# Two blocks of the w3 fold transposed by TensorE instead of VectorE

## The chip, the cores and the metric

The kernel runs on one core of a Trainium2 chip. The metric is the device time of one execution in microseconds (us); a lower one is better. Five engines run side by side, each through its own queue in program order: TensorE (PE in the views; PEld is its weight load), VectorE (DVE), ScalarE (ACT), GpSimd (POOL) and SyncE (SP, which here issues loads). "SPq" is SP's queue of DMA issues.

## The reference

Three layers follow each other: a kernelised attention over 8 heads, then a gated layer with four weight matrices, then a dense mixture of four experts. The change lies in the second.

```python
def _moe_ref(x, w1, w2, w3, w_out):
    a = x @ w1
    b = x @ w2
    h = a * b @ w3
    return (h @ w_out).astype(np.float32)
```

The sizes are x 1152x512, w1 and w2 512x1024, w3 1024x1024, w_out 1024x512. The weights arrive as float64.

## The kernel before

Since nothing stands between w3 and w_out, the kernel multiplies these two weights first ("the fold"): w3 @ w_out is 1024x512, half as wide as w3. It does this while the attention is still running, about 60 to 133 us into the span, in pieces that stand between the attention's own steps. The table `BESIDE` says which pieces go with which step; the framework's scheduler then sets the order of each engine's queue.

Every product here is done with numbers split in two float32r parts (HI and LO): three matmuls in place of one. `split` makes the parts: ScalarE copies the source to HI, VectorE subtracts HI from the source to get LO.

The fold needs w3 with its columns on the partitions, so w3 must be transposed. It has 8 row groups `m` of 128 rows, each cut in two halves `hf` of 512 columns: sixteen blocks, numbered u = 2m + hf. I call them u0 to u15. A block goes through these steps (line numbers of before):

1. SP loads it as float64, 512 KB, in four pieces of 32 partitions (L91), into one of six buffers `hx`.
2. ScalarE (L119, "the Prelu") and VectorE (L120 a shift, L121 an or) make it float32 in `w3f`, a tile of the tag `f64f`, which has two buffers.
3. VectorE transposes 32x32 squares (L257, STREAM_TRANSPOSE) from `w3f` to `w3t`. The four load pieces had put the rows where these squares give a whole transpose.
4. `split` makes `w3T` from `w3t`: ScalarE L83, VectorE L84. `w3T` has two buffers.
5. TensorE multiplies it with eight tiles of w_out: 12 matmuls of 128x512 a block (L274), 24 a fold of one `m`.

`fold(m)` sums in PSUM bank `po` for even m and `w` for odd m. The block ahead is prepared while the present one is multiplied. At the end of a fold `split` moves the bank's content into `w3o` (ScalarE L83, VectorE L84); only then may the bank be written again. During one fold the other fold's bank is the "spare bank".

Beside the fold run the attention steps of pairs 3 to 7: `features` (TensorE L394 into `ps_f`, VectorE L405 the maximum `mx`, ScalarE L407 eight exponentials `eq` or `ek`), transposes by TensorE (L134 into `ps_et` or `ps_x`), and the small products L360 and L565. After the fold come the gated products (L193, L224), which take what `load_w12` prepares, the expert input, and then the experts.

Of the kernel before, what the change touches and what calls it, by code (L numbers as in the profile page):

```python
# [10 lines left out]
F32R = mybir.dt.float32r  # L11
# [5 lines left out]
HI, LO = 0, 1  # L17
# [2 lines left out]
HALVES = 5  # L20
EARLY = 2
WARM = 6


PASSES = ((LO, HI), (HI, LO), (HI, HI))
# [21 lines left out]
def attention_moe_kernel(ctx: ExitStack, tc: tile.TileContext, q, k, v, omega, mw1, mw2, mw3, mwo, probs, ew1, ew2, out):  # L47
# [6 lines left out]
    P = 128  # L54
    SQ = 32
# [22 lines left out]
    def bank(tag):  # L78
        return ps_p.tile([P, 512], F32, tag=tag, name="ps_" + tag, bufs=BANKS[tag])

    def split(hi, lo, src, eng=None):

        high = nc.scalar.activation(out=hi, in_=src, func=ACTF.Copy)  # L83
        low = (eng or nc.vector).tensor_tensor(out=lo, in0=src, in1=hi.bitcast(F32), op=ALU.subtract)  # L84
        return high.ins, low.ins
# [8 lines left out]
    ahead, blocks = [], []  # L94

    def fetch(n):

        while len(ahead) < min(n, len(blocks)):
            r = hx_p.tile([P, 2, S], U32, tag="hx", name="f64").rearrange("p a s -> p (a s)")[:, :1024]
            ahead.append(load_f64(r.rearrange("p (c w) -> p c w", w=2), blocks[len(ahead)]))  # L100

    def next_block(name):

        n = next(turns)
        f = from_f64(ahead[n], name)
        fetch(n + 1 + HX_BUFS)
        return f
# [3 lines left out]
    def from_f64(r, name):  # L111


        low, high = r[:, :, 0], r[:, :, 1]
        f = cv.tile([P, 512], F32, tag="f64f", name=name, bufs=2)
        e = cv.tile([P, 512], U32, tag="f64e", name="f64e", bufs=2)
        fb = f.bitcast(U32)

        nc.scalar.activation(out=f, in_=high.bitcast(F32), func=ACTF.Prelu, scale=2.0**-112, alpha=2.0**32)  # L119
        nc.vector.tensor_scalar(out=e, in0=low, scalar1=29, scalar2=None, op0=ALU.logical_shift_right)  # L120
        nc.vector.scalar_tensor_tensor(out=fb, in0=fb, scalar=3, in1=e, op0=ALU.logical_shift_left, op1=ALU.bitwise_or)  # L121
        return f
# [10 lines left out]
    def transpose(out, in_, rows=slice(0, P)):  # L133
        return nc.tensor.transpose(out, in_, ident[rows, rows])  # L134
# [25 lines left out]
    cv = cctx.enter_context(tc.tile_pool(name="cv", bufs=2, side="right"))  # L160
# [80 lines left out]
    w3T = []  # L241
    for n in range(KF):
        hf, g = divmod(n, 4)
        blocks.append([mwo[hf * 512:(hf + 1) * 512].rearrange("(p g) d -> g p d", g=4)[g].unsqueeze(1)])
    for u in range(2 * KF):
        m, hf = divmod(u, KF // 4)
        rows = mw3[m * P:(m + 1) * P].rearrange("(j r) f -> r j f", r=SQ)
        blocks.append([rows[:, :, f:f + P] for f in range(hf * 512, hf * 512 + 512, P)])
    blocks += [[gated_columns(src, g)] for g in range(EARLY) for src in (mw1, mw2)]

    def fold_transposed(u):

        r = next_block("w3f")
        t = cv.tile([P, 512], U32, tag="f64e", name="w3t", bufs=2).bitcast(F32)
        nc.vector.transpose(t, r.rearrange("p (j c g) -> p j g c", j=4, g=4))  # L257
        t = t.rearrange("p (j g r) -> p g j r", j=4, g=4)
        wt = cv.tile([P, 2, 512], F32R, tag="w3T", name="w3T", bufs=2)
        hi, lo = (wt[:, x].rearrange("p (g j r) -> p g j r", j=4, g=4) for x in (HI, LO))  # L260
        split(hi, lo, t)
        w3T.append(wt)

    def fold(m):

        po = bank(("po", "w")[m % 2])
        n = 0
        for hf in range(KF // 4):
            u = m * (KF // 4) + hf
            while len(w3T) < min(u + 2, KF * (KF // 4)):  # L270
                fold_transposed(len(w3T))
            for g in range(4):
                for a, c in PASSES:
                    nc.tensor.matmul(  # L274
                        out=po, lhsT=w3T[u][:, a, g * P:(g + 1) * P], rhs=wo[hf * 4 + g][:, c],
                        start=(n == 0), stop=(n == 3 * KF - 1),
                    )
                    n += 1
        t = w3_p.tile([P, 2, 512], F32R, tag="w3o", name="w3o", bufs=KF)
        split(t[:, HI], t[:, LO], po)  # L280
        w3o.append(t)
# [57 lines left out]
    with ExitStack() as actx:  # L339
# [81 lines left out]
        ps = bank("po")  # L421
        for n in range(WARM):
            nc.tensor.matmul(out=ps, lhsT=zeros[:, :P], rhs=zeros, start=True, stop=True)
# [18 lines left out]
        for b in range(B):  # L442
            t = st.tile([P, H, D1], F32, name=f"vt{b}")
# [137 lines left out]
        def pair(n):  # L581
            return pairs[n] if 0 <= n < len(pairs) else None
# [34 lines left out]
        for n in range(len(pairs) + 1):  # L617
            u, u1, nx, nx2 = pair(n), pair(n - 1), pair(n + 1), pair(n + 2)
# [381 lines left out]
```

## Time and profile before

| | |
|---|---|
| median of 3 runs | 655.72 us (654.99 to 656.09) |
| the profiled execution | 656.22 us |
| its span, first to last instruction | 654.5 us |
| TensorE busy | 641.4 us, 98% of the span |
| VectorE busy | 460.8 us, 70% |
| ScalarE busy | 416.5 us, 64% |
| granted TensorE clock | 1.00 in all 40 slices |

The span is 1.7 us shorter than the execution's own time, which is what lies around it. The busy shares are means over stages with different limits. A TensorE that is busy is not at its peak, and its waits are few and short; so the stretches and the single waits have to be read.

### The profile page before, as it was taken

To read this page: it belongs to the slowest core of one execution; us is meant where nothing else is said; L and a number is where in the kernel's file an instruction comes from. 1 tells how busy PE (TensorE), PEld (TensorE's weight loads), DVE (VectorE), ACT (ScalarE), POOL (GpSimd) and SP (SyncE) were. 2 spreads that over 40 slices of the span, in tenths; PEclk is the share of its full clock that TensorE was granted. 3 is DMA by queue.
4 is the path that set the end of the run, shared out by engine and by line. 5 is a ranking of instruction groups with operands and counts; after the bars stand their busy time and mean duration, and the time that the engine had idled before them with its cause. 6 is when DMAs were issued, how large, how long until landed. Compare 5 with 4: busy or idle time off the path is not lost.

```text
span 654.5 us, 12627 instructions
## 1 busy us (share of the span) xinstructions
PE 641.4 (98%) x4971; PEld 609.8 (93%) x4971; DVE 460.8 (70%) x756; ACT 416.5 (64%) x892; POOL 122.6 (19%) x145
## 2 busy tenths in 40 slices
PE   8998999999999999999999999999999999999997
PEld 6787787789999999999999999999999999999997
DVE  3678987896623252657958968788598679687795
ACT  5899566664532242457868767778687677687750
POOL 2223000051310000000131330430422413314200
PEclk9999999999999999999999999999999999999999
DMA  9978662144200012002243672781783854836824
GB/s 258 326 192 229 167 166 70 34 129 146 81 0 1 1 66 65 1 2 65 64 138 106 106 134 69 151 153 19 146 146 46 150 111 83 140 86 96 165 63 146
DMA packets 58396, 70.61 MB, mean 108 GB/s; under 512 B 8864, under 2 KB 43680, under 8 KB 58336
## 3 DMA queue, kind: packets, MB, share of 16 engines
q1 hardware_dynamic: 44720, 48.79, 25.4%
q0 software_dynamic: 12640, 20.19, 20.4%
q8 instruction: 39, 0.64, 0.4%
q10 hardware_dynamic: 976, 0.82, 0.4%
q14 instruction: 21, 0.17, 0.1%
HBM read 47.24 MB, written 22.54 MB: 107 GB/s over the span
## 4 chain that ended last, share of the span: by engine, by line
PE 85%; ACT 5%; DVE 4%; DMA 3%; issue 2%; POOL 1%; SPq 0%; DVEq 0%; ACTq 0%; POOLq 0%
PE ps_f L823 7%; PE ps_f L908 6%; PE ps_et L823 3%; PE ps_po L823 3%; PE ps_w L823 3%; PE ps_x L823 3%; PE ps_kv L823 3%; PE ps_t L823 3%; PE ps_et L908 3%; PE ps_x L908 3%; PE ps_kv L908 3%; PE ps_w L908 3%; PE ps_t L908 3%; PE ps_po L908 3%; PE ps_f L224 3%
## 5 line engine op out<-in xcount | busy, mean ns | idle before, releaser
L857 POOL DMA_DIRECT2D out_dram<-o x98 | 82.1, 944 | 352.9 <-DVE o L883 170.1
L84 DVE TENSOR_TENSOR hs<-hd,hs 128x1024 fp32r<-128x1024 f32 x48 | 58.5, 1220 | 0.8 <-ACT hs L83 0.8
L83 ACT ACTIVATE hs<-hd 128x1024 fp32r<-128x1024 f32 x48 | 50.6, 1057 | 7.9 <-PE ps_et L908 2.5
L823 PE MATMUL ps_f<-x,w1e 128*128 128x288 f32 x288 | 46.9, 294 | 0.0
L807 ACT ACTIVATE hd<-hd 128x288 f32<-128x288 f32 x96 | 41.0, 437 | 7.9 <-DVE hd L805 7.3
L719 DVE TENSOR_TENSOR hd<-hd 128x512 f32<-128x512 f32 x64 | 44.0, 687 | 1.5 <-ACT hd L807 0.4
L719 DVE TENSOR_TENSOR raw<-raw 128x512 f32<-128x512 f32 x64 | 44.0, 687 | 0.6
L84 DVE TENSOR_TENSOR w2e<-raw,w2e 128x1024 fp32r<-128x1024 f32 x32 | 38.8, 1218 | 6.1 <-ACT w2e L83 6.0
L908 PE MATMUL ps_f<-w2e,hs 128*128 128x256 f32 x288 | 42.7, 282 | 0.0
L823 PEld LDWEIGHTS ps_f<-x,w1e 128*128 128x128 f32 x288 | 41.1, 188 | 0.2
L908 PEld LDWEIGHTS ps_f<-w2e,hs 128*128 128x128 f32 x288 | 38.2, 191 | 0.1
L83 ACT ACTIVATE w2e<-raw 128x1024 fp32r<-128x1024 f32 x32 | 32.9, 1056 | 6.1 <-DVE raw L719 3.7
L84 POOL TENSOR_TENSOR w<-w12f,w 128x512 fp32r<-128x512 f32 x16 | 22.2, 1396 | 67.9 <-ACT w L83 66.0
L84 DVE TENSOR_TENSOR w1e<-raw,w1e 128x1024 fp32r<-128x1024 f32 x24 | 29.3, 1222 | 4.4 <-ACT w1e L83 4.3
L83 ACT ACTIVATE hid<-a 128x192 fp32r<-128x192 f32 (+2 forms) x32 | 13.4, 441 | 27.0 <-DVE a L234 25.0
L83 ACT ACTIVATE w1e<-raw 128x1024 fp32r<-128x1024 f32 x24 | 25.4, 1060 | 4.6 <-DVE raw L719 2.9
L274 PE MATMUL ps_w<-wo,w3T 128*128 128x512 f32 x96 | 24.3, 400 | 2.3 <-DVE w3T L84 2.3
L376 DVE TENSOR_REDUCE mx<-ps_f 128x4 f32<-128x512 f32 x24 | 16.5, 689 | 13.7 <-PE ps_f L370 12.7
L274 PE MATMUL ps_po<-wo,w3T 128*128 128x512 f32 x96 | 24.0, 399 | 1.6 <-DVE w3T L84 1.6
L880 ACT ACTIVATE o<-ps_f,pr 128x256 f32<-128x256 f32 (+1 forms) x37 | 17.8, 482 | 9.9 <-PE ps_f L908 8.8
L823 PE MATMUL ps_et<-x,w1e 128*128 128x288 f32 x144 | 23.6, 295 | 0.0
L823 PE MATMUL ps_po<-x,w1e 128*128 128x288 f32 x144 | 23.6, 294 | 0.0
(307 smaller groups left out, 1709.7 us busy)
## 6 DMA issues: line engine op xcount, KB each, us to landing
raw<-in_moe_w_dram SPq DMA_DIRECT2D x32, 512.0 KB, 5.5
out_dram<-o POOLq DMA_DIRECT2D x56, 256.0 KB, 4.8
f<-in_moe_w_dram SPq DMA_DIRECT2D x64, 128.0 KB, 3.5
f<-in_moe_w_dram SPq DMA_DIRECT2D x16, 512.0 KB, 4.1
out_dram<-o POOLq DMA_DIRECT2D x42, 128.0 KB, 4.6
f<-in_moe_w_out_dram SPq DMA_DIRECT2D x8, 512.0 KB, 7.6
vr<-in_v_dram SPq DMA_DIRECT2D x8, 256.0 KB, 5.3
o<-out_dram SPq DMA_DIRECT2D x8, 256.0 KB, 5.3
```

What stands on the lines that cost most here:

```text
L83: high = nc.scalar.activation(out=hi, in_=src, func=ACTF.Copy)
L84: low = (eng or nc.vector).tensor_tensor(out=lo, in0=src, in1=hi.bitcast(F32), op=ALU.subtract)
L224: nc.tensor.matmul(out=ps[:, :third], lhsT=w12[w, g][:, x, kk], rhs=xb[kk][:, y, cols[c]], start=(kk == 0 and n == 0), stop=(kk == KD - 1 ...
L274: nc.tensor.matmul(out=po, lhsT=w3T[u][:, a, g * P:(g + 1) * P], rhs=wo[hf * 4 + g][:, c], start=(n == 0), stop=(n == 3 * KF - 1),)
L376: top = nc.vector.tensor_reduce(out=mx, in_=pv, op=ALU.max, axis=AX.X, negate=True)
L719: nc.vector.tensor_tensor(out=o, in0=x, in1=y, op=op)
L807: nc.scalar.activation(out=h, in_=src, func=ACTF.Relu)
L823: nc.tensor.matmul(out=ps, lhsT=w1t[a][:, x, kk, g * P:(g + 1) * P], rhs=x2[b, kk][:, y, s], start=(k in "125" and kk == 0 and n == 0), st ...
L857: dma = nc.gpsimd.dma_start(out=out[toks, d], in_=src[rows], **({} if fresh else dict(accum_op=ALU.add))).ins
L880: nc.scalar.activation(out=o, in_=ps, func=ACTF.Copy, scale=pr[:, t, e:e + 1])
L908: nc.tensor.matmul(out=ps, lhsT=t[a][:, x, g, j * P:(j + 1) * P], rhs=w2t[b][:, y, g], start=(k in "15" and g == 0 and n == 0), stop=(k in ...
```

## The change

Blocks u1 and u3 (the second halves of row groups 0 and 1) take another way. They are loaded in plain rows, in one DMA of 128 partitions in place of four of 32. Steps 1 and 2 are otherwise as before. In step 3 TensorE transposes them, four transposes of 128x128 into the spare bank: `w` for u1 (fold 0 sums in `po`), `po` for u3 (fold 1 sums in `w`). Each takes every fourth column of `w3f` as its stationary operand. `split` then reads the bank in place of `w3t`. The other 14 blocks are untouched.

```diff
+BY_PE = (1,3,)
...
     for u in range(2 * KF):
         m, hf = divmod(u, KF // 4)
-        rows = mw3[m * P:(m + 1) * P].rearrange("(j r) f -> r j f", r=SQ)
+        rows = mw3[m * P:(m + 1) * P]
+        if u in BY_PE:
+            blocks.append([rows[:, hf * 512:(hf + 1) * 512].unsqueeze(1)])
+            continue
+        rows = rows.rearrange("(j r) f -> r j f", r=SQ)
...
         r = next_block("w3f")
+        if u in BY_PE:
+            t = bank(("w", "po")[(u // 2 + 1 - u % 2) % 2])
+            for g in range(4):
+                transpose(t[:, g * P:(g + 1) * P], r.rearrange("p (c g) -> p g c", g=4)[:, g])
+            wt = cv.tile([P, 2, 512], F32R, tag="w3T", name="w3T", bufs=2)
+            split(wt[:, HI], wt[:, LO], t)
+            w3T.append(wt)
+            return
```

The scheduler orders the queues anew from there on. The diff moves the line numbers of what follows by 1 near `split` and by 13 from `fold` on. Three places show what moves.

TensorE's queue from the first twelve matmuls of fold 0 (block u0) on; `ps_po<-wo,w3T` and `ps_w<-wo,w3T` are the folds, `ident,xs` and `ident,eq` transposes of the attention. Before:

```order
L274 MATMUL ps_po<-wo,w3T 128x512 x12
L565 MATMUL ps_x<-kva,eTt 64x65 x8
L394 MATMUL ps_f<-omh,qT 128x128 x8
L274 MATMUL ps_po<-wo,w3T 128x512 x12
L274 MATMUL ps_w<-wo,w3T 128x512 x12
L134 MATMUL ps_et<-ident,xs 128x128 x2
L274 MATMUL ps_w<-wo,w3T 128x512 x12
```

Now:

```order
L287 MATMUL ps_po<-wo,w3T 128x512 x12
L135 MATMUL ps_w<-ident,w3f 128x128 x4
L578 MATMUL ps_x<-kva,eTt 64x65 x8
L407 MATMUL ps_f<-omh,qT 128x128 x8
L287 MATMUL ps_po<-wo,w3T 128x512 x12
L287 MATMUL ps_w<-wo,w3T 128x512 x12
L135 MATMUL ps_et<-ident,xs 128x128 x2
L135 MATMUL ps_po<-ident,w3f 128x128 x4
L287 MATMUL ps_w<-wo,w3T 128x512 x12
```

The transposes of u1 stand one step ahead of the fold of u1; those of u3 stand directly ahead of the fold of u3.

ScalarE's queue around the end of fold 0, with tile numbers and the semaphores that each instruction waits for: `w3o` is the copy of fold 0's bank, `w3f_1082` is the Prelu of u5, `w3f_1109` that of u6, `w3T_1036` is the copy of u3, `w3T_1063` that of u4. Before:

```order
L83 ACTIVATE w3o_863<-ps_po_793 128x512 [waits PE_49]
L83 ACTIVATE w3T_1036<-w3t_1034 128x512 [waits DVE_49,Activation_49]
L119 ACTIVATE w3f_1082<-f64_785 128x512 [waits DMAHW2_49,DMAHW3_49,DMAHW1_49,DMAHW0_49]
L83 ACTIVATE xt0_78<-ps_et_1012 128x64 [waits PE_49]
L83 ACTIVATE w3T_1063<-w3t_1061 128x512 [waits DVE_49,Activation_49]
L119 ACTIVATE w3f_1109<-f64_799 128x512 [waits DMAHW6_49,DMAHW7_49,DMAHW5_49,DMAHW4_49]
```

Now:

```order
L84 ACTIVATE w3o_860<-ps_po_787 128x512 [waits PE_49]
L120 ACTIVATE w3f_1082<-f64_779 128x512 [waits DMAHW4_49,DMAHW3_49,DMAHW5_49,DMAHW2_49,DVE_49]
L84 ACTIVATE xt0_78<-ps_et_1009 128x64 [waits PE_49]
L120 ACTIVATE w3f_1109<-f64_793 128x512 [waits DMAHW6_49,DMAHW1_49,DMAHW7_49,DMAHW0_49,DVE_49]
L84 ACTIVATE w3T_1036<-ps_po_1031 128x512 [waits PE_49,Activation_49]
L84 ACTIVATE w3T_1063<-w3t_1061 128x512 [waits Activation_49]
```

The copy of u3 stood right behind that of fold 0's bank; now it stands behind the Prelus of u5 and u6, and these two wait for VectorE, which they did not. While u3 lies untransposed in one of the two `f64f` buffers, u4, u5 and u6 take turns in the other: the Prelu of u6 waits for VectorE's transpose of u5 (`w3t_1092` below).

VectorE's queue there now, from the transpose of u4 on:

```order
L270 STREAM_TRANSPOSE w3t_1061<-w3f_1051 128x512
L121 TENSOR_SCALAR f64e_1083<-f64_779 128x512
L85 TENSOR_TENSOR w3o_860<-ps_po_787,w3o_860 128x512
L122 SCALAR_TENSOR_TENSOR w3f_1082<-w3f_1082,f64e_1083 128x512
L270 STREAM_TRANSPOSE w3t_1092<-w3f_1082 128x512
L85 TENSOR_TENSOR xt0_78<-ps_et_1009,xt0_78 128x64
L85 TENSOR_TENSOR w3T_1036<-ps_po_1031,w3T_1036 128x512
L85 TENSOR_TENSOR w3T_1063<-w3t_1061,w3T_1063 128x512
```

The subtraction of u3 comes behind the transposes of u4 and u5, while before it followed u3's own transpose and fold 0's subtraction.

TensorE's queue around the features of a later pair (`ps_f<-omh,qT`), from the second block of fold 4 (u9, `po`) on; `w` is fold 5, whose first block is u10. Before:

```order
L274 MATMUL ps_po<-wo,w3T 128x512 x12
L134 MATMUL ps_x<-ident,xs 128x128 x4
L274 MATMUL ps_w<-wo,w3T 128x512 x7
L394 MATMUL ps_f<-omh,qT 128x128 x8
L360 MATMUL ps_kv<-kva,eT 64x65 x3
L360 MATMUL ps_x<-kva,eT 64x65 x8
L360 MATMUL ps_kv<-kva,eT 64x65 x5
L274 MATMUL ps_w<-wo,w3T 128x512 x5
L134 MATMUL ps_et<-ident,eq 128x128 x4
```

Now, from behind u8 and u9, which are the row of 24:

```order
L287 MATMUL ps_w<-wo,w3T 128x512 x12
L135 MATMUL ps_x<-ident,xs 128x128 x4
L407 MATMUL ps_f<-omh,qT 128x128 x8
L373 MATMUL ps_kv<-kva,eT 64x65 x8
L373 MATMUL ps_x<-kva,eT 64x65 x8
L135 MATMUL ps_et<-ident,eq 128x128 x4
```

Five matmuls of u10, which stood between the features and the transposes of `eq`, are now ahead of the features, and the transposes of `xs` stand directly ahead of them.

## Rows read from the trace of the kernel before

**Rows 1.** The page's first part: busy us, share of the span, instructions.

```profile
PE 641.4 (98%) x4971; PEld 609.8 (93%) x4971; DVE 460.8 (70%) x756; ACT 416.5 (64%) x892; POOL 122.6 (19%) x145
```

**Rows 2.** Windows: busy us of PE, PEld, DVE, ACT, POOL; clock, DMA share, GB/s.

```profile
60.00:80.00 20.00, 18.02 (x137) 14.40 (x136) 19.72 (x35) 13.11 (x33) 1.66 (x2) 1.00 0.76 183
...
280.00:655.00 375.00, 370.30 (x2848) 365.23 (x2846) 285.96 (x416) 261.97 (x512) 82.05 (x98) 1.00 0.52 104
```

**Rows 3.** TensorE's waits from 40 to 142 us: in total, times, longest.

```profile
PE ps_w L274 <- DVE w3T L84: 2.3, 3, 1.1
PE ps_po L274 <- DVE w3T L84: 1.6, 3, 0.7
```

**Rows 4.** Its longest wait from 136 us to the end, same columns.

```profile
PE ps_t L193 <- POOL w L84: 0.7, 1, 0.7
```

**Rows 5.** Timeline of TensorE: start, duration, instruction, [idle before <-releaser]; u1 to u5.

```profile
68.21 3.01 PE L274 MATMUL ps_po<-wo,w3T 128*128 128x512 f32 x12 [0.69 <-DVE w3T L84]
71.06 2.89 PE L274 MATMUL ps_w<-wo,w3T 128*128 128x512 f32 x12
73.78 0.38 PE L134 MATMUL ps_et<-ident,xs 128*128 128x128 f32 x2
74.78 3.06 PE L274 MATMUL ps_w<-wo,w3T 128*128 128x512 f32 x12 [0.61 <-DVE w3T L84]
...
80.80 3.02 PE L274 MATMUL ps_po<-wo,w3T 128*128 128x512 f32 x12 [0.24 <-DVE w3T L84]
```

**Rows 6.** VectorE's groups from 55 to 142 us: busy us, mean ns.

```profile
L257 DVE STREAM_TRANSPOSE w3t<-w3f 128x512 f32<-128x512 f32 x16 | 17.5, 1097 | 0.2
...
L121 DVE SCALAR_TENSOR_TENSOR w3f<-w3f,f64e 128x512 uint32<-128x512 uint32 x16 | 11.4, 715 | 4.8 <-ACT w3f L119 4.4
L84 DVE TENSOR_TENSOR w3T<-w3t,w3T 128x512 fp32r<-128x512 f32 x16 | 10.9, 681 | 1.6 <-ACT w3T L83 1.6
```

**Rows 7.** Timeline of VectorE: the transpose of u1, and the maxima of a pair.

```profile
64.24 1.08 DVE L257 STREAM_TRANSPOSE w3t<-w3f 128x512 f32<-128x512 f32 x1
...
70.13 1.28 DVE L405 TENSOR_REDUCE mx<-ps_f 128x4 f32<-128x512 f32 x2
```

**Rows 8.** Timeline of ScalarE: the copy behind that transpose, and fold 0's copy.

```profile
65.36 0.64 ACT L83 ACTIVATE w3T<-w3t 128x512 fp32r<-128x512 f32 x1 [0.26 <-DVE w3t L257]
...
71.86 0.62 ACT L83 ACTIVATE w3o<-ps_po 128x512 fp32r<-128x512 f32 x1
```

**Rows 9.** The chain that ended last: start, duration, what; four transposes.

```profile
101.05 0.44 PE ps_x L134 x4
```

**Rows 10.** TensorE's weight loads from 40 to 142 us, those of transposes: mean ns.

```profile
L134 PEld LDWEIGHTS ps_et<-ident,eq 128*128 128x128 f32 x48 | 5.7, 140 | 1.3
```

**Rows 11.** TensorE's groups from 56 to 142 us, the same transposes: mean ns.

```profile
L134 PE MATMUL ps_et<-ident,eq 128*128 128x128 f32 x32 | 5.1, 280 | 0.0
```

**Rows 12.** Waits in SP's queue from 45 to 142 us, the longest.

```profile
SPq L91 <- DVE f64e L120: 44.0, 11, 20.5
```

**Rows 13.** Timeline of TensorE from the features at 103 us to fold 5's second block, u11.

```profile
101.24 1.86 PE L274 MATMUL ps_w<-wo,w3T 128*128 128x512 f32 x7
103.04 1.16 PE L394 MATMUL ps_f<-omh,qT 64*128 64x128 f32 x16
...
105.26 1.44 PE L274 MATMUL ps_w<-wo,w3T 128*128 128x512 f32 x5
106.54 0.60 PE L134 MATMUL ps_et<-ident,eq 128*128 128x128 f32 x4
...
111.34 0.96 PE L274 MATMUL ps_w<-wo,w3T 128*128 128x512 f32 x3 [0.61 <-DVE w3T L84]
```

**Rows 14.** Timeline of VectorE behind those features.

```profile
104.23 1.29 DVE L405 TENSOR_REDUCE mx<-ps_f 128x4 f32<-128x512 f32 x2 [1.22 <-PE ps_f L394]
```

**Rows 15.** Timeline of ScalarE behind those.

```profile
104.96 2.19 ACT L407 ACTIVATE eq<-ps_f,mx 128x128 f32<-128x128 f32 x8 [2.78 <-DVE mx L405]
106.98 1.32 ACT L119 ACTIVATE w3f<-f 128x512 f32<-128x512 f32 x2
```

## The prediction

> **What bounds the kernel now.** I read the shares first, then the windows, then TensorE's waits, then the timeline at each wait. TensorE is busy for 98% of the span [rows 1]. That is a mean over two regimes. From 280 us on it is busy for 370.3 of 375 us [rows 2], and its longest wait from 136 us to the end is 0.7 us [rows 4]. So whatever TensorE has lost or won when the fold ends, about 133 us, it still has at the end; nothing later gives it back. In the fold's first 20 us the tighter engine is VectorE: 19.72 us busy of 20, against TensorE's 18.02 [rows 2]. There TensorE waits for the transposed blocks: six waits from 40 to 142 us, 3.9 us in all, every one ended by VectorE's subtraction into `w3T` [rows 3]. Three of them stand near the change: 0.69 us ahead of u1, 0.61 ahead of u3, 0.24 ahead of u5 [rows 5]. One more, 0.61 ahead of u11, will matter [rows 13]. The granted clock is 1.00 throughout, the 2.4 GHz level [rows 2].
>
> The question is therefore when `w3T` of u1 and u3 is ready on the new way, and where TensorE's queue stands by then. I follow the queues in the clock of the trace of before.
>
> **What is removed, added and moved.** VectorE loses two transposes of 1.10 us [rows 6]. TensorE gets eight transposes; four that follow each other hold the chain for 0.44 us [rows 9], so 0.88 us. Both splits stay: a copy from a bank takes ScalarE 0.62 us and one from SBUF 0.64 [rows 8], the subtraction stays at 0.68 [rows 6]. From one engine to the next it takes 0.04 us: the transpose of u1 ends at 64.24 + 1.08 = 65.32 [rows 7] and its copy starts at 65.36 [rows 8]. SP issues six DMAs fewer. I cost that at nothing: SP's queue itself waits 44.0 us for VectorE to release load buffers [rows 12], so the loads run ahead, and none of the waits in [rows 3, 6] ends on a transfer. If that cover were gone, the copies would start later, which would only add to what follows.
>
> The price of a transpose can be taken otherwise. One takes 280 ns from start to end [rows 11], though the next starts 110 ns after it. The Trainium skill, "TensorE: Matmul & The Clock Gate", Part 4: PE-mode transpose, gives about 275 ns for one in a kernel's context. If that were paid one after the other, eight would be an estimated 2.2 us and the sum below 1.3 us higher. The row of one agrees with the page; the row of four says they overlap.
>
> **Block u1.** Its transposes stand behind the fold of u0, two steps ahead of the fold of u1. TensorE waited 0.69 us there [rows 5], so the 0.44 us can lie in that wait. If `w3T` is no later than before, the cost is 0; if the wait stays whole, 0.44. The copy of u1 now needs TensorE's result and has other work of ScalarE ahead of it. I take +0.2: the fold of u1 starts at 68.4 and that of u2 at 71.26, not 71.06.
>
> **Block u3.** Here is the main loss. The spare bank for u3 is `po`, which holds fold 0 until ScalarE has copied it (71.86 [rows 8]) and VectorE has subtracted. The order puts the transposes of u3 behind the twelve matmuls of u2 and two transposes of the attention, directly ahead of the fold of u3. With u2 at 71.26 the two transposes start 2.72 us later [rows 5], at 73.98, and take half of 0.44 us; u3's start at 74.2. The last of the four starts 0.33 us later and ends at 74.8. Behind that come copy (0.62), subtraction (0.68) and three hand-overs, with nothing else in the way: the fold of u3 could start at 76.2. Before it started at 74.78 [rows 5]. So +1.4 us is the lower bound at this place, for the order alone.
>
> Both engines have other work ahead of it. VectorE: the maxima of the pair (70.13 + 0.2, 1.28 long [rows 7]) to 71.6; u4's transpose (1.10) to 72.7; fold 0's subtraction, whose copy has come (71.86 + 0.2 + 0.62), to 73.4; the or of u5 (0.72 [rows 6]) to 74.1; u5's transpose to 75.2. ScalarE: the Prelu of u6 waits for that transpose, since u3 blocks the other `f64f` buffer; it takes half of 1.32 us [rows 15], to 75.9; only then the copy of u3, to 76.5; VectorE's subtraction, to 77.2. The fold of u3 starts at 77.2, +2.4 us. Durations overlap a little on one engine, which I leave in the rounding. Bounds: +1.4, and +3 if ScalarE's small attention copies come between.
>
> **Block u5.** Its transpose is done before u3's split, so u4's twelve matmuls cover what is left of it. The 0.24 us wait [rows 5] goes: -0.2. Behind u5 TensorE is 2.2 us late.
>
> **The features at 103 us.** From the features at 103.04 a chain runs to u11, the second block of fold 5, at 111.34 [rows 13]: maxima from 104.23 [rows 14], eight exponentials from 104.96, then the Prelus from 106.98 [rows 15], VectorE's steps of u11, and TensorE waiting 0.61 us at its end [rows 13]. It is 8.30 us long whatever TensorE does meanwhile. Five matmuls of u10, which filled part of it (105.26 to 106.54, 1.28 us [rows 13]), now stand ahead of the features. So the chain starts 1.3 us later and TensorE waits for `eq` inside it: +1.3. Bounds: 0, if something else had set u11, and 1.3. Further, the transposes of `xs` now stand directly ahead of the features, and their split ahead of the maxima on VectorE. Counted from the start of the features: about 0.2 (the last transpose's 280 ns less 110) + 0.62 + 0.68 = 1.5 us, where the maxima began after 1.19 (104.23 - 103.04): +0.3. Bounds 0 and 0.7, the whole subtraction.
>
> **The sum.** +2.4 - 0.2 + 1.3 + 0.3 = +3.8 us at u11. The fold's order behind it is as before, so this stands until the fold's end, and TensorE's fullness carries it to the last store. The profiled execution's own time of 656.2 gives 660.0; it lies 0.5 us over the median of 655.72, so the median becomes 659.5 us.
>
> **Rivals.** *Relief (faster).* VectorE is the tight engine and loses 2.2 us of work. If all three near waits closed, 0.69 + 0.61 + 0.24 = 1.54 us, less 0.88 for the transposes: -0.7, 655.0 us. For: 19.72 of 20 us busy. Against: u3's new way is longer than its old one. It decides if `w3T` of u3 is ready when its transposes end, 74.8; by the rows above it is 1.4 us late at best. 0.08.
>
> *Only the added work.* The waits keep their 3.9 us and TensorE has 0.88 us more: 656.6 us. For: TensorE is the fullest engine. Against: the lateness of u3 does not depend on it. 0.12. The Trainium skill, "Perfetto Trace Analysis", section Identifying the Most-Contended Engine, says to improve the engine with the highest occupancy first, which speaks against a change that loads TensorE to relieve VectorE; by it alone 656.6 would come out. In the stretch of the change VectorE is the fuller engine [rows 2], so the trace bears the rule out only in part.
>
> *Only u3.* The later reordering costs nothing, because u9 and u10 also come later and the chain to u11 has slack I do not see: +2.2, 657.9 us. 0.15.
>
> *Slow stationary reads.* Every fourth element of `w3f` is read as weights; no row shows a strided weight load. Bounds: the contiguous load's 140 ns [rows 10], and four times that if each element costs what four did, 0.42 us more a load, 1.7 a block. I take the contiguous one, the nearest row. At the upper end u1's transposes overflow the wait and add 1.0, u3's copy comes 0.5 later beyond that: 661.0 us. 0.13.
>
> That the change does not do what it says is out: the order shows both blocks on TensorE.
>
> **How the numbers follow.** The forecast has 0.52, with its own range 658.4 to 660.7 (u3 between +1.4 and +3). The range 656.8 to 661.3 leaves out relief and added work alone, 0.20. A change under 0.2%, 1.3 us, is about what a measurement cannot tell from none (the three runs spread over 1.1 us). Faster: relief, 0.08. Same: added work alone, 0.12. Slower: 0.52 + 0.15 + 0.13 = 0.80.
>
> **What would show it.** Right: a wait of about 2.4 us ahead of the fold of u3 in place of 0.61, ended by VectorE's `w3T`; on ScalarE the copy of u3 behind u6's Prelu; no wait ahead of u5; waits of about 1 us for `eq` ahead of the transposes near 107 us; from 140 us on the same work, some 3.8 us later. The first fails if u3's fold starts within 1 us of u2's end; the third if the transposes of `eq` follow without a wait. Weight loads of the new transposes well over 140 ns would speak for the last rival. Wrong altogether if the waits of the fold shrink below 3 us in sum, or if the gated products start as early as now.

## The result, and the profile after

The changed kernel takes 662.83 us in the median of four runs (661.82 to 663.30), the kernel before, run beside it, 655.56 (654.99 to 656.09). The ratio is 1.0109 with a 95% interval of 1.0097 to 1.0121: slower by 7.3 us, where +3.8 was forecast. The profiled execution took 662.65 us, its span 660.9.

The page of the changed kernel, TensorE's busy line and two lines of the span in 40 slices of 16.5 us:

```profile
PE 643.7 (97%) x4979; PEld 611.8 (93%) x4979; DVE 456.6 (69%) x754; ACT 415.3 (63%) x892; POOL 122.3 (19%) x145
...
PE   8998899999999999999999999999999999999997
...
PEclk9999899999999999999999999999999999999999
```

TensorE's share fell by a point against [rows 1], and one slice, the fifth (66 to 83 us), has an 8 for the granted clock. The windows show how deep that is; the number behind POOL's is the granted clock:

```profile
core 0: us, PE busy (x) PEld busy (x) DVE busy (x) ACT busy (x) POOL busy (x), PEclk, DMA share, GB/s
70.00:76.00 6.00, 4.15 (x22) 3.32 (x20) 4.86 (x9) 4.03 (x10) 0.00 (x0) 1.00 1.06 216
76.00:82.00 6.00, 5.60 (x18) 4.47 (x19) 3.65 (x9) 1.66 (x6) 0.00 (x0) 0.72 0.89 169
77.40:80.70 3.30, 3.30 (x9) 2.62 (x8) 1.92 (x5) 0.22 (x1) 0.00 (x0) 0.50 0.77 147
```

From 77.4 to 80.7 us TensorE has the lower of its two levels, 1.2 GHz. In [rows 2] nothing like it stands. TensorE's waits from 58 to 165 us, by what ended them (us in total, times, longest):

```profile
PE ps_w L287 <- DVE w3T L85: 3.8, 3, 2.2
PE ps_po L287 <- DVE w3T L85: 1.3, 2, 0.7
PE ps_et L135 <- ACT eq L420: 0.9, 2, 0.7
PE ps_t L225 <- ACT a L201: 0.8, 1, 0.8
PE ps_t L194 <- POOL w L85: 0.6, 1, 0.6
PE ps_x L578 <- DVE xt L85: 0.5, 1, 0.5
```

Against [rows 3, 4] three kinds are new: the wait of 2.2 us for `w3T`, the two for `eq`, and two of 0.8 and 0.5 us (L225, L578) that lie behind 140 us, where I had expected nothing. The timeline of TensorE puts them in place (L287 at 115.67 is the fold of u11):

```profile
61.90 3.03 PE L287 MATMUL ps_po<-wo,w3T 128*128 128x512 f32 x12 [0.66 <-DVE w3T L85]
...
67.71 3.01 PE L287 MATMUL ps_po<-wo,w3T 128*128 128x512 f32 x12 [0.61 <-DVE w3T L85]
70.56 2.89 PE L287 MATMUL ps_w<-wo,w3T 128*128 128x512 f32 x12
73.29 0.38 PE L135 MATMUL ps_et<-ident,xs 128*128 128x128 f32 x2
73.50 0.64 PE L135 MATMUL ps_po<-ident,w3f 128*128 128x128 f32 x4
76.40 4.61 PE L287 MATMUL ps_w<-wo,w3T 128*128 128x512 f32 x12 [2.25 <-DVE w3T L85]
80.84 2.92 PE L287 MATMUL ps_po<-wo,w3T 128*128 128x512 f32 x12
...
109.73 0.33 PE L135 MATMUL ps_et<-ident,eq 128*128 128x128 f32 x1 [0.23 <-ACT eq L420]
110.76 0.59 PE L135 MATMUL ps_et<-ident,eq 128*128 128x128 f32 x3 [0.70 <-ACT eq L420]
...
115.67 3.02 PE L287 MATMUL ps_w<-wo,w3T 128*128 128x512 f32 x12 [0.60 <-DVE w3T L85]
...
139.96 1.87 PE L194 MATMUL ps_t<-xt,w 128*128 128x288 f32 x12 [0.63 <-POOL w L85]
...
150.08 0.69 PE L578 MATMUL ps_x<-kva,eTt 128*64 128x65 f32 x16 [0.53 <-DVE xt L85]
...
154.00 2.35 PE L225 MATMUL ps_t<-xt,w 128*128 128x384 f32 x12 [0.80 <-ACT a L201]
```

The two traces are laid side by side at the fold of u0, which starts at 61.90 us here and at 62.76 before. Counted from there the loss is:

| up to | before | after | loss in this stretch |
|---|---|---|---|
| fold of u3 starts | 74.78 | 76.40 | +2.48 |
| its twelve matmuls, to the next fold | 77.67 | 80.84 | +1.55 |
| fold of u11 starts | 111.34 | 115.67 | +1.16 |
| gated product that waits for GpSimd's `w` | 135.87 | 139.96 | -0.24 |
| last six matmuls start | 650.24 | 655.91 | +1.58 |

That is 6.53 us. The span grew by 6.4: the head was 0.86 shorter, and from the last matmul's end to the end of the span it took 4.1 us, not 3.4. The rest of the 7.3 is that the profiled execution lay 0.7 us over the median before and 0.2 under it after.

One of the four runs, the one of 661.82 us, has a granted clock of 1.00 over the whole execution; the other three (662.65, 663.01 and 663.30, the first of them the traced one) have 0.996 to 0.997. So the fall of the clock is not in every execution, and without it the change still costs over 6 us.

### The profile page after: what moved, and what is told of

Read it like the earlier page. It is cut to its first block, busy times and chain, and to the rows that moved or that the text cites. A ratio compares the mean times of both kernels' runs of the same rounds, so it can differ in the third digit from the quotient of the medians.

```text
span 660.9 us, 12626 instructions
## 1 busy us (share of the span) xinstructions
PE 643.7 (97%) x4979; PEld 611.8 (93%) x4979; DVE 456.6 (69%) x754; ACT 415.3 (63%) x892; POOL 122.3 (19%) x145
## 4 chain that ended last, share of the span: by engine, by line
PE 83%; ACT 6%; DVE 5%; issue 2%; DMA 2%; POOL 1%; DVEq 0%; ACTq 0%
PE ps_f L836 7%; PE ps_f L921 6%; PE ps_et L836 3%; PE ps_po L836 3%; PE ps_w L836 3%; PE ps_x L836 3%; PE ps_kv L836 3%; PE ps_t L836 3%; PE ps_et L921 3%; PE ps_x L921 3%; PE ps_kv L921 3%; PE ps_w L921 3%; PE ps_t L921 3%; PE ps_po L921 3%; PE ps_f L225 3%; PE ps_w L287 3%
## 5 line engine op out<-in xcount | busy, mean ns | idle before, releaser
L287 PE MATMUL ps_w<-wo,w3T 128*128 128x512 f32 x96 | 26.1, 421 | 3.8 <-DVE w3T L85 3.8
L287 PEld LDWEIGHTS ps_w<-wo,w3T 128*128 128x128 f32 x96 | 18.4, 198 | 8.3 <-DVE w3T L85 4.3
L389 DVE TENSOR_REDUCE mx<-ps_f 128x4 f32<-128x512 f32 x24 | 16.5, 688 | 13.0 <-PE ps_f L383 11.9
L287 PE MATMUL ps_po<-wo,w3T 128*128 128x512 f32 x96 | 23.8, 398 | 1.3 <-DVE w3T L85 1.3
```

What stands on the lines that cost most here:

```text
L287: nc.tensor.matmul(out=po, lhsT=w3T[u][:, a, g * P:(g + 1) * P], rhs=wo[hf * 4 + g][:, c], start=(n == 0), stop=(n == 3 * KF - 1),)
L389: top = nc.vector.tensor_reduce(out=mx, in_=pv, op=ALU.max, axis=AX.X, negate=True)
```

## The experiments

The theory after the traces: u3 comes late; the wait that this makes lets the clock fall; and behind it ScalarE's and VectorE's queues stand in an order that makes TensorE wait twice more in the gated stage. The rivals: the transposes on TensorE as such, with their strided reads or their loads, cost the time; u1 shares the loss; the late bank, not ScalarE's queue, makes u3 late; the loads of the gated columns are simply late for a TensorE that comes later. Where nothing else is said, an experiment edits the changed kernel. Times are medians, with ratios to the kernel before run on the same chip.

**Filling the wait.** Eight matmuls on a zero operand (`ZEROS` is 8) behind the last of u3's transposes, `turned[3]`.

```diff
...
+            for _ in range(ZEROS if u == 3 else 0):
+                with tc.issue_after(turned[3].ins):
+                    nc.tensor.matmul(out=po, lhsT=zero, rhs=wo[0][:, HI], start=False, stop=False)
             for g in range(4):
                 for a, c in PASSES:
```

> Changed kernel with eight matmuls on a zero operand (they add zero to fold 1's bank) directly behind the transpose of u3, in the 2.25 us in which TensorE waits; nothing else stands in another place. Theory (the granted clock fell to 0.5 because TensorE stood still in that wait): no stretch at 0.5 behind the wait, u3's twelve matmuls take about 3.0 us and not 4.61, the wait itself shrinks to under 0.8 us because zeros fill it, and the whole is 1.4 to 1.6 us shorter than the changed kernel, about 661.3 us. Rival (the clock falls at that place for another reason, such as the work of the whole chip up to there): a stretch at 0.5 as before, 662.8 us or up to 0.5 us more.

661.89 us, 1.0095 [1.0082, 1.0109]. Its timeline of TensorE, and the window from 76 to 82 us with the granted clock behind POOL's number:

```profile
73.94 0.64 PE L136 MATMUL ps_po<-ident,w3f 128*128 128x128 f32 x4
74.34 2.09 PE L290 MATMUL ps_w<-wo,zero 128*128 128x512 f32 x8
76.81 3.02 PE L293 MATMUL ps_w<-wo,w3T 128*128 128x512 f32 x12 [0.37 <-DVE w3T L86]
79.66 2.89 PE L293 MATMUL ps_po<-wo,w3T 128*128 128x512 f32 x12
```

```profile
76.00:82.00 6.00, 5.63 (x25) 4.32 (x25) 5.14 (x11) 2.22 (x7) 0.00 (x0) 1.00 0.81 180
```

u3's fold comes no earlier (14.5 us behind that of u0 in both traces), but its twelve matmuls take 3.02 us, not 4.61, and the granted clock is 1.00 from 70 to 82 us. With the idle time filled the fall is gone: the idle time was its cause here. The twelve matmuls return 1.59 us, up to the next fold; but the fold of u0 starts 0.39 later in this trace, so that the span is 1.2 shorter. The median is 0.9 shorter, less than the 1.4 to 1.6 expected. The loss behind 140 us is whole.

**The Prelu, the bank, and both with an earlier place.** Three runs on why u3 is late. First, u6's Prelu held behind u3's copy, `copied[3]`:

```diff
...
-        f = from_f64(ahead[n], name)
+        with tc.issue_after(copied[3]) if n == KF + 6 else nullcontext():
+            f = from_f64(ahead[n], name)
```

> Changed kernel with one ScalarE instruction in another place: u6's Prelu stands behind u3's copy, not ahead of it. Theory (u3 is late because its copy stands behind that Prelu, which waits for VectorE's transpose of u5): the wait ahead of u3's fold falls from 2.25 to about 1.4 us, and the whole by that 0.85 us, and by up to 1.5 us more if the shorter wait leaves the clock at its upper level: 660.5 to 662.0 us. Rival (the bank, free only when fold 0 is out of it, is what makes u3 late): the wait stays within 0.3 us of 2.25, 662.8 us.

Second, only another bank, which frees u3's transposes of fold 0's evacuation:

```diff
-            t = bank(("w", "po")[(u // 2 + 1 - u % 2) % 2])
+            t = bank("w" if u == 1 else "x")
```

> Changed kernel with the transpose of u3 put into bank x, which is free there, in place of bank po. The transpose then stands ahead of the two transposes of xs, still behind u2's twelve matmuls; u6's Prelu stays ahead of u3's copy. Theory (the Prelu on ScalarE ends the wait, not the bank): the wait stays within 0.3 us of 2.25, time 662.3 to 663.0 us. Rival (the bank is what makes it late): the wait falls under 1.5 us, 660.5 to 662.0 us.

Third, both edits, and the second half of u2's matmuls behind the transposes:

```diff
...
+                  with tc.issue_after(turned[3].ins) if u == 2 and g > 1 else nullcontext():
                     nc.tensor.matmul(
                         out=po, lhsT=w3T[u][:, a, g * P:(g + 1) * P], rhs=wo[hf * 4 + g][:, c],
```

> Changed kernel with three things at u3: the transpose goes into bank x, it stands between the sixth and the seventh of u2's twelve matmuls, and u6's Prelu stands behind u3's copy. Theory (a wait of 2.25 us and a stretch at half clock behind it, both from where u3's work stands): the wait falls to about 1.1 us, because u3's subtraction then stands behind VectorE's transpose of u5, there is no stretch at 0.5, and the time is 2.3 to 2.8 us under the changed kernel, 660.0 to 660.5 us; what is left over 655.6 is the added work of TensorE and the later places that changed. Rival (the clock falls with any new wait there): 661.5 us.

660.52 us (1.0075 [1.0063, 1.0088]), 663.24 (1.0118 [1.0102, 1.0133]) and 659.87 (1.0071 [1.0058, 1.0084]). The fold of u3 on TensorE in the three, in this order:

```profile
75.62 3.03 PE L288 MATMUL ps_w<-wo,w3T 128*128 128x512 f32 x12 [1.47 <-DVE w3T L85]
```

```profile
76.97 4.24 PE L287 MATMUL ps_w<-wo,w3T 128*128 128x512 f32 x12 [2.27 <-DVE w3T L85]
```

```profile
75.46 3.06 PE L289 MATMUL ps_w<-wo,w3T 128*128 128x512 f32 x12 [0.83 <-DVE w3T L85]
```

The bank alone does nothing: 2.27 us of wait with it free, at 0.2 us more than the 662.3 to 663.0 expected. u3's transposes still stand behind u2's twelve matmuls there, and u6's Prelu ahead of u3's copy. The third run is a little better than expected, with 0.83 us of wait for 1.1, and the clock is 1.00. The Prelu alone takes 0.78 us off the wait, and at 1.47 us the clock stays up, so the median falls by 2.3. What is left of the wait is the new way itself: in that trace copy and subtraction follow directly on the transposes (74.25 to 75.57), and the fold on them. ScalarE's rows in the changed kernel show what it had done:

```profile
74.47 0.66 ACT L120 ACTIVATE w3f<-f 128x512 f32<-128x512 f32 x1 [0.54 <-DVE w3t L270]
75.03 0.58 ACT L84 ACTIVATE w3T<-ps_po 128x512 fp32r<-128x512 f32 x1
```

The Prelu waits for VectorE's transpose of u5, and the copy of u3 stands behind it, although the transposes of u3 end at 74.14. Nor did the bank hold these back: VectorE's subtraction of fold 0 ends at 72.69, and they start at 73.50.

**Which block.** Two runs with one block each.

```diff
-BY_PE = (1,3,)
+BY_PE = (3,)
```

> Only u3 goes through TensorE, u1 as in the kernel before. TensorE's order behind u3's fold is that of the changed kernel. Theory (u3 carries nearly all: its wait, the half clock behind it, the five matmuls ahead of the features and the order of the gated stage; u1 carries under 0.5 us): the wait ahead of u3's fold is 2.2 to 2.8 us, the granted clock falls to 0.5 behind it, 662.0 to 663.3 us. Rival (u1 and u3 share the loss by half): 658.5 to 660.0 us.

```diff
-BY_PE = (1,3,)
+BY_PE = (1,)
```

> Only u1 goes through TensorE, u3 as in the kernel before. u3's fold comes without a long wait and TensorE's order further on is another one than in either kernel, with three transposes of eq that follow closely on each other. Theory: no stretch at half clock, a wait under 1 us at u1's fold, about 0.7 us of added transposes with it, and up to 1.5 us in the moved transposes of eq: 656.3 to 658.5 us. Rival (u1 and u3 share the loss by half): 658.5 to 660.0 us.

u3 alone: 662.28 us, 1.0106 [1.0092, 1.0120], nearly the whole loss, with a wait of 2.75 us and a fall of the clock. The wait at that place comes about otherwise there: u3's copy stands ahead of u6's Prelu and ends at 74.1 us, but VectorE's subtraction stands behind its transpose of u5 (74.29 to 75.37) and starts at 75.30. So in the changed kernel ScalarE's Prelu makes the wait longer than the new way needs; with u3 alone VectorE's queue does. u1 alone: 658.90, 1.0052 [1.0039, 1.0066]. That misses the expected 656.3 to 658.5 and lies in the rival's range, but not for the rival's reason, for u3 alone has 6.9 us of the 7.3. TensorE of u1 alone at 87 to 98 us:

```profile
87.30 0.66 PE L135 MATMUL ps_et<-ident,eq 128*128 128x128 f32 x4 [0.69 <-ACT eT L552]
...
92.74 0.66 PE L135 MATMUL ps_et<-ident,eq 128*128 128x128 f32 x4 [1.52 <-ACT eT L552]
93.69 4.60 PE L287 MATMUL ps_w<-wo,w3T 128*128 128x512 f32 x12 [0.29 <-DVE w3T L85]
```

The same 4.60 us for twelve matmuls, at another place and behind other waits; the granted clock from 94.8 to 98.0 us is 0.58. The transposes of `eq`, drawn together by the new order, make the waits, which I had counted; the clock that goes with them I had not. So u1 is not cheap by itself: its loss is another one, which the two-block order happens to avoid. The theory could have named it.

**Other blocks.** u0 and u2 go into the bank of the fold that comes next, free in that time; then u0 alone.

```diff
-BY_PE = (1,3,)
+BY_PE = (0,2,)
```

> Two blocks again, but u0 and u2, whose transposes go into the bank of the fold that comes next, which is free for the whole of the fold before. Theory (the loss comes from the bank and the queue at u3, and not from transposes on TensorE as such): no wait over 0.5 us at u3's fold, no stretch at half clock, VectorE's freed time takes the waits at u1 away: 655.0 to 656.5 us, the same as before within 0.2%. Rival (eight transposes on TensorE and the order of the later stages cost it whichever block is taken): 658 us or more.

```diff
-BY_PE = (1,3,)
+BY_PE = (0,)
```

> One block, u0, whose transpose goes into bank po ahead of all folds, where TensorE has waits of its own. Theory: the added 0.6 us lies in time in which TensorE waits, and no wait is added: 654.7 to 656.0 us, the same as before or up to 0.1% faster. Rival (any block put on TensorE costs its 0.6 us and reorders what follows): 656.2 us or more.

656.51 us, 1.0013 [1.0004, 1.0022], and 655.65, 1.0004 [0.9995, 1.0013]; the clock is 1.00 in both. The first is 1.2 us slower, at the upper edge of what was expected; the second cannot be told from the kernel before. Eight transposes on TensorE, with the same strided reads and plain loads, need not cost 7 us, nor 2. But nothing is won either: TensorE waited before u0's fold anyway, and with u0 on TensorE it still waits, longer than the 0.68 us of before:

```profile
59.39 0.75 PE L135 MATMUL ps_po<-ident,w3f 128*128 128x128 f32 x4
...
63.65 2.56 PE L287 MATMUL ps_po<-wo,w3T 128*128 128x512 f32 x10 [1.29 <-DVE w3T L85]
```

**The kernel before, only late.** No transposes on TensorE at all: u3's split is done twice, then four times, with the same values (the edit for two; four has a 4 in place of the 2).

```diff
-        split(hi, lo, t)
+        for _ in range(2 if u == 3 else 1):
+            split(hi, lo, t)
```

> The kernel before, with no transposes on TensorE and no other loads: only the split of u3 is done twice, with the same values, so that u3 comes about 1.6 us later to its fold. TensorE's order behind it then becomes nearly that of the changed kernel (u10 whole ahead of the features at 103 us, the other order in the gated stage). Theory (the loss of the changed kernel is that of a late u3: its wait, the half clock behind it, and an order of the later stages made for a later TensorE): a wait of about 2.2 us ahead of u3's fold, a stretch at 0.5 behind it, u3's twelve matmuls 4.4 to 4.7 us, and 660.5 to 662.5 us. Rival (the transposes on TensorE with their reads, or the loads in plain rows, are needed for the clock's fall or for the later waits): no stretch at 0.5, 657 to 658.5 us.

> The kernel before with the split of u3 done four times, with the same values: u4's fold then goes ahead of u3's, TensorE waits about 3 us once ahead of it, and all further on stands in the order of the kernel before. Theory: the wait brings the clock down once (a stretch at 0.5, about 1.5 us lost in the twelve matmuls behind it), and the later stages lose nothing: 655.5 + 2.0 (3.0 less the two waits of 1.1 and 0.7 that it takes in, with 0.8 for the work that stands beside) + 1.5 = 658.3 to 659.8 us. Rival (a late TensorE loses in the later stages whatever the order): 660.5 us or more. Without a fall of the clock: 657.5 us or less.

Twice: 660.35 us, 1.0074 [1.0061, 1.0088]. Four times: 658.25, 1.0043 [1.0031, 1.0056]. Both lie just under what was expected (660.5 and 658.3 us at the least). The waits of TensorE in the first, then in the second the two folds behind the wait, u4's and u3's:

```profile
PE ps_w L275 <- DVE w3T L84: 3.7, 3, 2.2
PE ps_po L275 <- DVE w3T L84: 1.4, 2, 0.7
PE ps_t L224 <- ACT a L200: 0.9, 1, 0.9
PE ps_et L134 <- ACT eq L408: 0.9, 2, 0.7
PE ps_t L193 <- POOL w L84: 0.6, 1, 0.6
PE ps_x L566 <- DVE xt L84: 0.5, 1, 0.5
```

```profile
75.92 4.47 PE L275 MATMUL ps_po<-wo,w3T 128*128 128x512 f32 x12 [3.01 <-DVE w3T L84]
80.23 2.88 PE L275 MATMUL ps_w<-wo,w3T 128*128 128x512 f32 x12
```

The first list is that of the changed kernel, wait for wait, within 0.1 us. A u3 that is late makes the wait, the fall of the clock (4.57 us for the twelve matmuls), the late features and both waits of the gated stage, without one transpose on TensorE. In the stretches of the table its trace has +1.58, +1.48, +1.27, -0.28 and +1.72, in sum 5.77 us of the 6.53. The changed kernel has 0.90 more up to the fold of u3, 0.3 of it at u1, whose transposes hold TensorE for 0.56 us (64.76 to 65.32); behind it, the sums agree within 0.14.

The median has less, 5.1 us of the 7.3, and for a reason that the trace does not show: three of the five runs (660.03 to 660.35) have a granted clock of 1.00 over the execution, the other two (660.89, and 661.04 with the trace) have 0.997. With the same edit the clock falls in one execution and not in the next; how long the wait was where it did not fall, no trace shows.

The second has the wait and the clock, but the later order of before. Counted from the fold of u0 it is 3.26 us late at the features (105.06) and 3.26 at the last six matmuls (652.26): nothing is lost behind the fold. So a TensorE that is late by this much loses nothing there; the other order does. The rival on late loads falls by this for a TensorE 3.3 us late; the next experiment answers it at the full lateness of the changed kernel.

**The gated stage.** ScalarE's and VectorE's rows of the changed kernel ahead of the two new waits:

```profile
152.90 0.66 ACT L120 ACTIVATE w12f<-f 128x512 f32<-128x512 f32 x1 [1.61 <-POOL w L85]
153.46 0.39 ACT L201 ACTIVATE a<-ps_t 128x288 f32<-128x288 f32 x1
```

```profile
148.61 0.82 DVE L121 TENSOR_SCALAR f64e<-f 128x512 uint32<-128x512 uint32 x1 [1.88 <-DMA f<-in_moe_w_dram]
149.35 0.68 DVE L85 TENSOR_TENSOR xt<-ps_x,xt 128x512 fp32r<-128x512 f32 x1
```

On both engines a step of the column loads waits, for GpSimd or for a transfer, with TensorE's own next input behind it. In the kernel before the copy out of `ps_t` stood ahead of that Prelu:

```profile
144.23 0.39 ACT L200 ACTIVATE a<-ps_t 128x288 f32<-128x288 f32 x1
...
147.66 0.68 ACT L119 ACTIVATE w12f<-f 128x512 f32<-128x512 f32 x1 [1.40 <-POOL w L84]
```

The edit holds two Prelus back, one behind the copy of the last attention output (`split[0]`), one behind that out of `ps_kv` (`last_a`), which follows the one out of `ps_t`:

```diff
...
-        nc.scalar.activation(out=f, in_=high.bitcast(F32), func=ACTF.Prelu, scale=2.0**-112, alpha=2.0**32)
+        with tc.issue_after(behind) if behind else nullcontext():
+            nc.scalar.activation(out=f, in_=high.bitcast(F32), func=ACTF.Prelu, scale=2.0**-112, alpha=2.0**32)
...
-                f = from_f64(r, "w12f")
+                f = from_f64(r, "w12f", {(3, 0): pairs[-1].split[0], (4, 0): last_a.get((0, 1))}.get((g, w)))
...
```

> Changed kernel, with two Prelus of ScalarE held back in the gated stage: that of the third streamed column group behind the copy of the last attention output, that of the fourth behind the copies of the second gated group. TensorE's five inputs of the tail then stand where nothing waits. Up to 140 us nothing is changed. Theory (the two waits of 0.5 and 0.8 us at 150 and 154 us come from the order in which ScalarE and VectorE stand there): both waits gone, 1.0 to 1.6 us shorter than the changed kernel, 661.2 to 661.9 us. Rival (the loads of the column groups come late to TensorE's pace and the wait only moves on): 662.5 us or more.

661.14 us, 1.0087 [1.0073, 1.0100]. All engines from 140 to 160 us, TensorE's busy time first, this kernel and then the changed one:

```profile
140.00:160.00 20.00, 20.00 (x157) 19.71 (x158) 15.45 (x40) 11.45 (x26) 6.49 (x5) 1.00 0.65 208
```

```profile
140.00:160.00 20.00, 18.67 (x145) 18.14 (x146) 15.01 (x35) 11.03 (x25) 6.82 (x5) 1.00 0.68 211
```

Both waits are gone, 20.00 us busy of 20. From the gated product that waits for `w` to the last six matmuls it takes 514.46 us, where the kernel before took 514.37 and the changed one 515.95: 1.49 of the 1.58 of the table come back. The median is 1.7 us lower; taken each against the kernel before that ran beside it, the loss is 5.9 us in place of 7.3, 1.4 less.

**The features.** u10's last five matmuls go back behind the features, whose last matmul is `feat[-1]`.

```diff
...
+                  with tc.issue_after(feat[-1]) if u == 10 and n > 6 else nullcontext():
                     nc.tensor.matmul(
                         out=po, lhsT=w3T[u][:, a, g * P:(g + 1) * P], rhs=wo[hf * 4 + g][:, c],
```

> Changed kernel, with the last five of u10's twelve matmuls held behind the features at 107 us, as they stood in the kernel before; u12's last five go behind the next features by the same rule, and the gated stage's order changes with it. Theory (the five matmuls ahead of the features cost 1.3 us): no wait for eq there, the fold of u11 starts 1.0 to 1.4 us earlier, 661.2 to 661.8 us if the gated stage keeps its loss, down to 660.0 us if it loses that too. Rival (u11 is late for another reason): 662.5 us or more.

662.06 us, 1.0097 [1.0083, 1.0111]. From the fold of u3 (76.68) to that of u11 (114.94) it takes 38.26 us where the changed kernel took 39.27: the 1.0 expected at the place. The wait for `eq` is gone, though one of 0.77 us for `xs` has come in. But the edit also moved the queues behind it. At the gated product that waits for `w` 0.66 of the 1.0 is left, and from there to the last six matmuls it takes the 515.95 us of the changed kernel, with TensorE's wait for ScalarE's `a` now 1.2 us long. The median is 0.8 lower, 0.3 above the 661.2 to 661.8 expected. The step is right at its place; the whole is inconclusive on the rest.

## Why the prediction was half right

**The wait at u3: right, to 0.1 us.** Forecast +2.4, measured +2.48 from u0's fold, with a wait of 2.25 us for the 2.4 named. The reason was right where it named ScalarE's queue and VectorE's transpose of u5. The bank, which it named beside the order as what puts u3's transposes late, sets nothing: it was free 0.8 us before they started.

**u1 and u5: right.** +0.36 for +0.2, and no wait at u5.

**The features: right at 1.4 for 1.6.** The +1.16 of the table is this with the -0.24 of u5's wait. The waits for `eq` are 0.93 us. The chain from the features to u11 takes 8.42 us for 8.30, so the term of 0.3 for the transposes of `xs` measured 0.1.

**The step that failed is the sum**: "the fold's order behind it is as before, so this stands until the fold's end, and TensorE's fullness carries it to the last store". What I had summed measured 3.64 us at u11 (2.48 and 1.16) for 3.8. But the sum took two things as unchanged without showing it: the price of the matmuls behind the new wait, and the order of all queues behind the fold. So two terms were missing:

- *The clock, +1.55.* I read 1.00 throughout the trace of before and put matmuls at that price behind a wait more than twice as long as the longest there (1.1 us [rows 3]). The runs: filled wait, no fall; late u3 without transposes, the same fall. The Trainium skill, "TensorE: Matmul & The Clock Gate", section HAM oscillation, tells of matmuls that start at the lower clock after each wait for data. The trace agrees in part: it has the fall once, with twelve matmuls 1.55 us longer, but the first of them still run at 1.00 (76.4 to 77.3 us), and one of the four runs has no fall.
- *The gated stage, +1.58.* I took the stage behind 140 us as the same work in the same order. TensorE's work was the same; ScalarE's and VectorE's queues were not, and the prediction does not follow them beyond the fold. Two Prelus put back return 1.49 of it.

The forecast's own range, 658.4 to 660.7, does not follow from the bounds named with it: u3 at +1.4 and +3 gives 658.5 and 660.1.

Of the rivals, relief and added work fell as reckoned. "Only u3" fell: the features did cost their share. Slow stationary reads fell. The weight loads of the new transposes are longer than the 140 ns of the other transposes [rows 10], 204 to 207:

```profile
L135 PEld LDWEIGHTS ps_w<-ident,w3f 128*128 128x128 f32 x4 | 0.6, 204 | 0.1
```

But they overlap: four transposes hold TensorE for 0.40 us at u3 (73.94 to 74.34 in the run with zeros) and 0.56 at u1, where 0.44 was reckoned.

## What to carry to other kernels

A new wait on a full TensorE that is longer than any wait in the trace that left the clock alone may bring the lower clock to the matmuls behind it. Price both cases: here waits of 2.15 us and more did so in every trace, one of 1.47 did not. Where a schedule is made anew, compare the queues of all engines to the end of the program, not only where the edit stands: a block that came 1.6 us late cost 5.8 here, trace against trace, about half of it through other orders of the queues. And an engine with slack in its busy time, like ScalarE, still decides when the full one may go on, if an instruction that waits stands ahead of the one that is needed.

## What the chip showed that I had not expected

The granted clock fell behind waits of 2.15 to 3.01 us (seven traces), and stayed at 1.00 behind waits of 1.47 and 0.83 at the same place. But the one wait's length does not decide alone. With u1 alone it fell behind 1.52 us, with 0.69, 0.28 and 0.29 us of waits around it, and TensorE busy for 4.29 us from 87.0 to 93.5. And the same kernel can have the fall in one execution and not in another: by the granted clock of each run, one of four of the changed kernel has none, and three of five of the kernel before with u3's split done twice. Each fall cost about the same, 1.4 to 1.6 us over the matmuls behind it.

The weight loads of the new transposes, 128 by 128 with a stride of four elements, take 204 to 207 ns, against 140 for those of the other transposes. The contiguous loads of the fold take 188 to 203 in the same stretch, so that no run shows the price of the stride alone.
